# Spreading the float64-to-float32 weight conversion and the head norms over more engines of one Trainium2 core

## The chip, the core and the metric

The kernel runs on one core of one Trainium2 chip. The core has five engines that run their own in-order instruction queues and meet through semaphores: TensorE (PE, matrix products into the accumulator memory PSUM), VectorE (DVE), ScalarE (ACT), GpSimd (POOL), and SyncE (SP, which here only issues DMAs). The metric is device time in microseconds (us) from one execution; the kernel before was run three times, with a median of 1260.8 us.

## What is computed

A linear attention with random features, and a gated feed-forward layer on its result. Cut to what matters:

```python
# q, k, v: 8 batches x 8 heads x 576 tokens x 64, omega: 128 x 64
def phi(x):
    proj = np.einsum('bhsd,md->bhsm', x, omega)
    sq = np.sum(x * x, axis=-1, keepdims=True) / 2.0
    h = proj - sq
    h = h - np.max(h, axis=-1, keepdims=True)
    return np.exp(h) / np.sqrt(m)
q_p, k_p = phi(q * scale), phi(k * scale)
kv = np.einsum('bhsm,bhsd->bhmd', k_p, v)
num = np.einsum('bhsm,bhmd->bhsd', q_p, kv)
den = np.einsum('bhsm,bhm->bhs', q_p, np.sum(k_p, axis=2))[..., None] + 1e-06
x = (num / den)                      # 4608 tokens x 512 after a transpose
gate = 1.0 / (1.0 + np.exp(-(x @ w_gate)))     # w_gate, w_val: 512 x 1536
val = x @ w_val
out = gate * val @ w_out                       # w_out: 1536 x 512
```

The three weight matrices come as float64. The kernel gets them as pairs of 32-bit words and turns each pair into one float32 itself, on the chip.

## The kernel before

**Precision.** Most matrix products are made of three: each float32 operand is split into a rounded part `hi` and a remainder `lo` (`split`, L68: ScalarE writes `hi` at L70, VectorE or GpSimd subtracts at L71), and TensorE multiplies lo with hi, hi with lo, and hi with hi.

**Stages.** While the attention runs (all tasks of `attention`, L681), TensorE's queue also holds the products of a first pass over the feed-forward layer (`first_pass`, L227, products `gv` at L247) for four of the twelve column tiles of the gate and value weights. When attention ends, the rest of the first pass follows, and then `second_pass` (L394, products `gw` at L351) does the other columns with a seven-product scheme for 2 x 2 blocks. Last, `last` (L443, products `po` at L465) multiplies by the output weights.

**Weight conversion.** `from_float64` (L74) converts one half tile, 128 partitions x 512 numbers. `bits` holds the low and high words side by side, so `lo` and `hi` are read with a step of two words. `a` is a scratch tile that both halves of a weight tile share, and `t` receives the float32. VectorE has six instructions (L78, L81, L85, L88, L92, L94): clear the sign, clamp, shift the exponent and mantissa into place, put back the sign, cut out the power of two (into `a`), and multiply the low word by it (back into `a`). GpSimd's add at L96 joins the parts. There are 36 such halves: 8 for the first pass (tiles named `e`), 22 for the weights of the second pass and the output (tiles `c`), and 6 for the last three weight tiles, which are converted after attention has ended because there was no room before (tiles `late`). For `c` and `late` tiles four GpSimd subtractions (L180) follow, and SyncE stores the result to DRAM (`w32`, L181), from where `unit` (L192) loads it later (L199, L200) and splits it (L214 on ScalarE, L215).

**Head norms.** `norms` (L493) loads one tile of 128 tokens x 512 (8 heads x 64) at a time, ScalarE squares it into `x2` (L501, two buffers), and VectorE sums each head's 64 squares (L503, 128 x 512 to 128 x 8). There are 72 such tiles. The scaled sums (`sq`, L507) enter `hm` (L556), from which keys take their bias `nb` (L574) for the exponentials `kpk` (L587), and queries take `sub` (L613) and `h` (L615), which TensorE transposes (`pt`, L626).

**Order.** Program code yields in turns from tasks, and a scheduler then sets each engine's order from that program and its own estimate of times; what is wrapped in `pin` (most of the second pass) keeps program order. SyncE's loads and stores share one in-order queue: the loads of attention inputs `raw` (L519), which wait until a buffer's split is done, the loads `xr` of attention output (L224), of weight words (L144), the stores L181, and the loads of `unit`.

Of the kernel before, what the change touches and what calls it, by code (L numbers as in the profile page):

```python
# [9 lines left out]
F32 = mybir.dt.float32  # L10
F32R = mybir.dt.float32r
AF = mybir.ActivationFunctionType
ALU = mybir.AluOpType
AX = mybir.AxisListType
U32 = mybir.dt.uint32

B, H, S, D = 8, 8, 576, 64
# [56 lines left out]
def from_float64(nc, t, a, bits):  # L74


    lo, hi = bits[:, :, 0], bits[:, :, 1]
    nc.vector.tensor_scalar(out=a, in0=hi, scalar1=0x7FFFFFFF, scalar2=None, op0=ALU.bitwise_and)  # L78

    f = a.bitcast(F32)  # L80
    nc.vector.tensor_scalar(  # L81
        out=f, in0=f, scalar1=LARGEST, scalar2=LEAST, op0=ALU.min, op1=ALU.max
    )

    nc.vector.tensor_scalar(  # L85
        out=t, in0=a, scalar1=3, scalar2=0x3FFFFFFF, op0=ALU.logical_shift_left, op1=ALU.bitwise_and
    )
    nc.vector.scalar_tensor_tensor(  # L88
        out=t, in0=hi, scalar=0xC0000000, in1=t, op0=ALU.bitwise_and, op1=ALU.bitwise_or
    )  # L90

    nc.vector.tensor_scalar(out=a, in0=t, scalar1=0xFF800000, scalar2=None, op0=ALU.bitwise_and)  # L92
    r = a.bitcast(F32)
    nc.vector.scalar_tensor_tensor(out=r, in0=lo, scalar=2.0**-52, in1=r, op0=ALU.mult, op1=ALU.mult)  # L94
    x = t.bitcast(F32)
    nc.gpsimd.tensor_tensor(out=x, in0=x, in1=r, op=ALU.add)  # L96


# [1 line left out]
def attn_glu_kernel(ctx: ExitStack, tc, qT, kT, qn, kn, va, om, ident, w, out):  # L100
    nc = tc.nc
# [36 lines left out]
    def converted(cv, i):  # L138


        raw = [cv[:, (1 + h) * 2 * WP : (2 + h) * 2 * WP] for h in range(2)]
        for h in range(2):
            o = i + h * WP
            nc.sync.dma_start(out=raw[h].rearrange("p (n two) -> p n two", two=2), in_=w[:, o : o + WP, :])  # L144
        yield
        for h in range(2):
            from_float64(
                nc, cv[:, h * WP : (h + 1) * WP], cv[:, 6 * WP :],
                raw[h].rearrange("p (n two) -> p n two", two=2),
            )  # L150
            yield
# [336 lines left out]
    def span(name, b):  # L488

        g = GROUPS[name][b]  # L490
        return g[0][0], g[-1][-1] + 1

    def norms(pool, name, u, b, src):  # L493

        t0, t1 = span(name, b)
        s = pool.tile([P, MID + 1, H], F32, tag="ss", bufs=2, name=f"ss{name}{u}_{b}")[:, : t1 - t0]
        for t in range(t0, t1):
            x = pool.tile([P, DM], F32, tag="nat", bufs=3, name=f"nat{name}{u}_{t}")
            nc.sync.dma_start(out=x, in_=src[u, :, t, :])
            x2 = pool.tile([P, DM], F32, tag="x2", bufs=2, name=f"x2{name}{u}_{t}")  # L500
            nc.scalar.activation(out=x2, in_=x, func=AF.Square)  # L501
            yield
            nc.vector.tensor_reduce(  # L503
                out=s[:, t - t0, :], in_=x2.rearrange("p (h d) -> p h d", d=D), axis=AX.X, op=ALU.add
            )
        sq = pool.tile([P, MID + 1, H], F32, tag="sq", bufs=6, name=f"sq{name}{u}_{b}")
        nc.vector.tensor_scalar(  # L507
            out=sq[:, : t1 - t0], in0=s, scalar1=SCALE * SCALE / 2.0, scalar2=None, op0=ALU.mult
        )
        sqs[name, u, b] = sq  # L510
        yield
# [158 lines left out]
    for u in range(U):  # L670
        for b in range(2):
            for n, x in (("k", kn), ("q", qn)):
                for p in range(NP):
                    if p == 1:
                        tasks.append((("n" + n, u, b), (), lambda pool, a=(n, u, b, x): norms(pool, *a)))
                    needs = (("k", u, p, b - 1),) if n == "k" and b else (("k", u, p, b), ("q", u - 1 + b, p, 1 - b)) if n == "q" else ()
                    make = keys if n == "k" else queries
                    tasks.append(((n, u, p, b), needs, lambda pool, a=(u, p, b), f=make: f(pool, *a)))
# [32 lines left out]
    with tc.tile_pool(name="early", bufs=1) as early:  # L711
# [39 lines left out]
        for n, _ in enumerate(gates):  # L751
# [9 lines left out]
            if n == left - 2 * NE:  # L761
                parts = operands(0)
                x = next(parts)
# [114 lines left out]
```

## Time and profile before

| | |
|---|---|
| three runs | 1260.8, 1253.29, 1263.12 us; median 1260.8 |
| the profiled execution's own time | 1255.57 us |
| its span, first to last instruction | 1253.8 us |
| share of the span: PE, DVE, ACT, POOL | 93%, 70%, 42%, 43% |
| mean granted TensorE clock | 0.967 of full |

The profile has three parts that matter here: tables of busy time in stretches of the span, lists of who waited for whom (an engine's idle time, put down to what ended it last), and the instructions in order of time. A busy TensorE is not one at its best: when its granted clock is lower, the same products are busy for longer. VectorE's 70% is a mean over stages that differ: the prediction reads it by stage.

### The profile page before, as it was taken

What the parts mean: (1) busy time and instruction counts of PE and PEld (TensorE: products, weight loads), DVE (VectorE), ACT (ScalarE), POOL (GpSimd) and SP (SyncE); (2) the same over time, 40 slices, a digit from 0 to 9 for tenths busy, and PEclk for the clock granted to TensorE, in tenths of its full rate; (3) what the DMA queues carried; (4) which work ended last, traced back from release to release, by engine and by line L of the source; (5) the groups of instructions that cost most, each with busy time, mean ns of one, the idle gap of its engine ahead of it and who ended that gap; (6) DMA issues with size and microseconds to landing.
All of it is one profiled execution on the core that took longest, in us unless ns stands there. A gap on an engine that the chain in (4) does not pass through costs nothing.

```text
span 1253.8 us, 23995 instructions
## 1 busy us (share of the span) xinstructions
PE 1171.8 (93%) x8828; PEld 1108.1 (88%) x8828; DVE 881.2 (70%) x1907; ACT 529.1 (42%) x1164; POOL 544.2 (43%) x599
## 2 busy tenths in 40 slices
PE   5789889999898999999799999999999899999998
PEld 5689868788877888788799999999998899999998
DVE  4889877999786565574866656665658786777773
ACT  5556755655444554331533222222224343434331
POOL 2554443755465232154366666666666311111110
PEclk7799889999898999999799999999999999999999
DMA  7666767775565330266532333233327676666662
GB/s 252 211 199 218 242 219 225 273 258 190 196 223 174 109 117 26 93 234 219 177 121 119 123 123 123 89 122 152 123 89 273 212 230 203 192 187 187 198 186 95
DMA packets 104950, 219.43 MB, mean 175 GB/s; under 512 B 11136, under 2 KB 42112, under 8 KB 103040
## 3 DMA queue, kind: packets, MB, share of 16 engines
q1 hardware_dynamic: 87984, 198.94, 47.9%
q10 hardware_dynamic: 16848, 18.95, 4.4%
q8 instruction: 70, 1.15, 0.4%
q14 instruction: 48, 0.39, 0.1%
HBM read 141.82 MB, written 76.02 MB: 174 GB/s over the span
## 4 chain that ended last, share of the span: by engine, by line
PE 48%; POOL 3%; issue 2%; DVE 2%; DMA 2%; ACT 0%; SPq 0%; DVEq 0%; POOLq 0%; ACTq 0%
PE gw L351 27%; PE po L465 21%; POOL late L180 1%; DMA ye<-ye 1%; DMA u<-w 1%; POOL late L96 1%; POOL xe L71 0%; DMA yl<-yl 0%; DMA yr<-yl 0%; POOL xl L296 0%; POOL u L215 0%; DVE yl L71 0%; DVE u L209 0%; POOL yl L391 0%; SPq L224 0%
## 5 line engine op out<-in xcount | busy, mean ns | idle before, releaser
L351 PE MATMUL gw<-xl,u 128*128 128x256 f32 x3024 | 366.4, 284 | 11.0 <-ACT xl L293 4.0
L351 PEld LDWEIGHTS gw<-xl,u 128*128 128x128 f32 x3024 | 364.3, 191 | 13.1 <-ACT xl L293 4.2
L465 PE MATMUL po<-u,yh 128*128 128x256 f32 x1512 | 272.5, 283 | 0.0
L465 PEld LDWEIGHTS po<-u,yh 128*128 128x128 f32 x1512 | 234.8, 191 | 0.0
L465 PE MATMUL po<-u,yl 128*128 128x256 f32 x756 | 214.1, 283 | 3.2 <-DVE yl L71 3.2
L247 PE MATMUL gv<-xe,wh 128*128 128x512 f32 (+1 forms) x640 | 199.9, 387 | 4.1 <-POOL xe L71 4.0
L70 ACT ACTIVATE yh<-yr 128x896 fp32r<-128x896 f32 x108 | 100.6, 951 | 156.5 <-PE po L465 88.2
L465 PEld LDWEIGHTS po<-u,yl 128*128 128x128 f32 x756 | 144.4, 191 | 3.8 <-DVE yl L71 3.8
L247 PEld LDWEIGHTS gv<-xe,wh 128*128 128x128 f32 x640 | 116.0, 193 | 22.1 <-POOL xe L71 6.6
L71 POOL TENSOR_TENSOR yl<-yr,yh 128x896 fp32r<-128x896 f32 x17 | 37.9, 2231 | 215.3 <-PE po L465 140.3
L247 PE MATMUL gv<-xe,wl 128*128 128x512 f32 (+1 forms) x320 | 124.5, 391 | 1.7 <-ACT xe L70 1.1
L71 DVE TENSOR_TENSOR yl<-yr,yh 128x896 fp32r<-128x896 f32 x91 | 99.5, 1102 | 37.8 <-PE po L465 24.9
L331 DVE TENSOR_TENSOR u<-gw,p 128x256 f32<-128x256 f32 x144 | 60.7, 422 | 60.6 <-PE gw L351 52.0
L595 PEld LDWEIGHTS pkv<-v,kpk 128*128 128x128 f32 x512 | 78.9, 212 | 24.4 <-ACT kpk L587 21.8
L595 PE MATMUL pkv<-v,kpk 128*128 128x66 f32 x512 | 85.7, 293 | 15.5 <-ACT kpk L587 14.3
L71 POOL TENSOR_TENSOR lok<-rawk,hik 128x256 fp32r<-128x256 f32 (+1 forms) x80 | 54.6, 700 | 96.4 <-ACT hik L70 96.2
L71 POOL TENSOR_TENSOR loq<-rawq,hiq 128x256 fp32r<-128x256 f32 (+1 forms) x80 | 57.2, 724 | 73.0 <-ACT hiq L70 72.3
L456 DVE TENSOR_TENSOR yr<-yr 128x128 f32<-128x128 f32 x144 | 64.8, 484 | 28.1 <-DMA yr<-ye 27.5
L71 POOL TENSOR_TENSOR xe<-xr,xe 128x512 fp32r<-128x512 f32 (+1 forms) x40 | 49.9, 1265 | 60.3 <-ACT xe L70 56.5
L587 ACT ACTIVATE kpk<-ppk,nb 128x128 f32<-128x128 f32 x256 | 69.6, 390 | 14.7 <-DVE nb L574 14.5
L638 PE MATMUL pnq<-kv,qpq 128*128 128x66 f32 (+1 forms) x640 | 71.1, 267 | 1.2 <-ACT qpq L628 1.2
L638 PEld LDWEIGHTS pnq<-kv,qpq 128*128 128x128 f32 (+1 forms) x640 | 67.3, 183 | 5.1 <-ACT qpq L628 3.1
(116 smaller groups left out, 2175.5 us busy)
## 6 DMA issues: line engine op xcount, KB each, us to landing
yl<-yl SPq DMA_DIRECT2D x36, 896.0 KB, 3.9
yr<-yl SPq DMA_DIRECT2D x72, 448.0 KB, 3.5
xr<-xT SPq DMA_DIRECT2D x68, 256.0 KB, 4.1
c<-w SPq DMA_DIRECT2D x22, 512.0 KB, 5.2
w<-c SPq DMA_DIRECT2D x11, 1024.0 KB, 5.0
v<-va SPq DMA_DIRECT2D x32, 330.0 KB, 3.5
natk<-kn SPq DMA_DIRECT2D x36, 256.0 KB, 4.4
natq<-qn SPq DMA_DIRECT2D x36, 256.0 KB, 3.8
```

The lines of the kernel that those rows point to most:

```text
L70: nc.scalar.activation(out=hi, in_=x, func=AF.Copy)
L71: (lo_engine or nc.vector).tensor_tensor(out=lo, in0=x, in1=hi.bitcast(F32), op=ALU.subtract)
L96: nc.gpsimd.tensor_tensor(out=x, in0=x, in1=r, op=ALU.add)
L180: nc.gpsimd.tensor_tensor(out=o, in0=x, in1=y, op=ALU.subtract)
L247: nc.tensor.matmul(gv, lhsT=u[:, s], rhs=v, start=(m == 0), stop=(m == 3 * KC - 1))
L331: return nc.vector.tensor_tensor(out=o, in0=a, in1=b, op=ALU.add)
L351: nc.tensor.matmul(o, lhsT=u[:, k, s], rhs=v[:, kc, :], start=(first and m == 0), stop=(m == 5), skip_group_check=not first,)
L456: nc.vector.tensor_tensor(out=raw[:, o], in0=raw[:, a], in1=raw[:, b], op=op)
L465: nc.tensor.matmul(o, lhsT=u[:, i, :], rhs=v[:, k, :], start=(j + m == 0 and n in (1, 6, 5, 4)), stop=(j == NPAIR - 1 and m == 2), skip_gr ...
L587: nc.scalar.activation(out=kp[t][:, h, :], in_=pp[:, 2 * i + h, :], func=AF.Exp, bias=nb[:, t - t0, h : h + 1], scale=SCALE,)
L595: nc.tensor.matmul(pkv[:, h, :], lhsT=kp[b * MID + i][:, h, :], rhs=v[:, i, h, :], start=(i == 0), stop=(i == MID),)
L638: nc.tensor.matmul(pn[r, 2 * i + h, :], lhsT=qp[:, 2 * i + h, r], rhs=kvs[u, p, bb][:, h, :], start=True, stop=True,)
```

## The change

Three edits.

1. In `from_float64`, the sign is cleared by ScalarE (the function Abs on the word read as float32) instead of VectorE.
2. In the same place, the multiplication of the low word by the power of two becomes two instructions: ScalarE converts and scales the low word in place (L94), GpSimd multiplies (L95), and its add (L96) follows.
3. In `norms`, GpSimd first adds the second 32 squares of each head to the first 32 (L504, 128 x 8 x 32, in place), and VectorE sums the 32 that are left (L505).

```diff
     lo, hi = bits[:, :, 0], bits[:, :, 1]
-    nc.vector.tensor_scalar(out=a, in0=hi, scalar1=0x7FFFFFFF, scalar2=None, op0=ALU.bitwise_and)
+    nc.scalar.activation(out=a.bitcast(F32), in_=hi.bitcast(F32), func=AF.Abs)
...
     nc.vector.tensor_scalar(out=a, in0=t, scalar1=0xFF800000, scalar2=None, op0=ALU.bitwise_and)
-    r = a.bitcast(F32)
-    nc.vector.scalar_tensor_tensor(out=r, in0=lo, scalar=2.0**-52, in1=r, op0=ALU.mult, op1=ALU.mult)
-    x = t.bitcast(F32)
+    r, small, x = a.bitcast(F32), lo.bitcast(F32), t.bitcast(F32)
+    nc.scalar.activation(out=small, in_=lo, func=AF.Copy, scale=2.0**-52)
+    nc.gpsimd.tensor_tensor(out=r, in0=small, in1=r, op=ALU.mult)
     nc.gpsimd.tensor_tensor(out=x, in0=x, in1=r, op=ALU.add)
...
-            nc.vector.tensor_reduce(
-                out=s[:, t - t0, :], in_=x2.rearrange("p (h d) -> p h d", d=D), axis=AX.X, op=ALU.add
-            )
+            x2 = x2.rearrange("p (h two d) -> p h two d", two=2, d=D // 2)
+            nc.gpsimd.tensor_tensor(out=x2[:, :, 0], in0=x2[:, :, 0], in1=x2[:, :, 1], op=ALU.add)
+            nc.vector.tensor_reduce(out=s[:, t - t0, :], in_=x2[:, :, 0], axis=AX.X, op=ALU.add)
```

The number of products on TensorE, of DMAs and of table loads stays what it was. The scheduler gives every engine a new order, though, since its estimates of times change. Two places show what that means.

The first is GpSimd's queue at the start of the program. `lok_1_0` is the remainder of keys of head pair 1 from tile 0 on, `x2k_0` the squares of key tile 0. Before:

```order
L71 TENSOR_TENSOR lok_1_0_117<-rawk_1_0_91,hik_1_0_116 128x256
L71 TENSOR_TENSOR lok_1_2_121<-rawk_1_0_91,hik_1_2_120 128x256
L71 TENSOR_TENSOR lok_1_4_125<-rawk_1_0_91,hik_1_4_124 128x128
L71 TENSOR_TENSOR lok_0_0_129<-rawk_0_0_84,hik_0_0_128 128x256
L71 TENSOR_TENSOR lok_0_2_133<-rawk_0_0_84,hik_0_2_132 128x256
L71 TENSOR_TENSOR lok_0_4_137<-rawk_0_0_84,hik_0_4_136 128x128
L71 TENSOR_TENSOR lok_2_0_277<-rawk_2_0_263,hik_2_0_276 128x256
```

The same place after:

```order
L504 TENSOR_TENSOR x2k_0_89<-x2k_0_89 128x8x32
L504 TENSOR_TENSOR x2k_1_97<-x2k_1_97 128x8x32
L71 TENSOR_TENSOR lok_1_0_122<-rawk_1_0_91,hik_1_0_121 128x256
L71 TENSOR_TENSOR lok_1_2_126<-rawk_1_0_91,hik_1_2_125 128x256
L71 TENSOR_TENSOR lok_1_4_130<-rawk_1_0_91,hik_1_4_129 128x128
L71 TENSOR_TENSOR lok_0_0_134<-rawk_0_0_84,hik_0_0_133 128x256
L71 TENSOR_TENSOR lok_0_2_138<-rawk_0_0_84,hik_0_2_137 128x256
L504 TENSOR_TENSOR x2k_2_103<-x2k_2_103 128x8x32
L504 TENSOR_TENSOR x2k_3_109<-x2k_3_109 128x8x32
L504 TENSOR_TENSOR x2k_4_115<-x2k_4_115 128x8x32
L71 TENSOR_TENSOR lok_0_4_142<-rawk_0_0_84,hik_0_4_141 128x128
```

Two additions of squares now stand ahead of the first remainder that TensorE needs, and three more behind it, ahead of the sums of the first group of keys.

The second place is GpSimd's queue between the end of attention and the second pass, where the last three weight tiles (three buffers of the tile `late`) are converted and the last inputs of the first pass (`xe`) are split. Before, from the second half of the second weight tile on:

```order
L71 TENSOR_TENSOR xe_2_7582<-xr_0_7435,xe_2_7582 128x512
L71 TENSOR_TENSOR xe_3_7585<-xr_0_7435,xe_3_7585 128x512
L96 TENSOR_TENSOR late_7247<-late_7247 128x512
L180 TENSOR_TENSOR late_7247<-late_7247 128x256 x3
L96 TENSOR_TENSOR late_7248<-late_7248 128x512
L180 TENSOR_TENSOR late_7247<-late_7247 128x256
L96 TENSOR_TENSOR late_7248<-late_7248 128x512
L180 TENSOR_TENSOR late_7248<-late_7248 128x256 x4
```

The same place after:

```order
L95 TENSOR_TENSOR late_7350<-late_7350 128x512
L71 TENSOR_TENSOR xe_1_7687<-xr_0_7542,xe_1_7687 128x512
L95 TENSOR_TENSOR late_7349<-late_7349 128x512
L96 TENSOR_TENSOR late_7350<-late_7350 128x512
L96 TENSOR_TENSOR late_7349<-late_7349 128x512
L71 TENSOR_TENSOR xe_2_7690<-xr_0_7542,xe_2_7690 128x512
L180 TENSOR_TENSOR late_7349<-late_7349 128x256 x3
L71 TENSOR_TENSOR xe_3_7693<-xr_0_7542,xe_3_7693 128x512
L180 TENSOR_TENSOR late_7349<-late_7349 128x256
L95 TENSOR_TENSOR late_7350<-late_7350 128x512
L96 TENSOR_TENSOR late_7350<-late_7350 128x512
L180 TENSOR_TENSOR late_7350<-late_7350 128x256 x4
```

The multiplications L95 are new in the queue, and the last splits `xe_2` and `xe_3` stand behind more of the conversion than before.

## The prediction

> **What bounds the kernel now.** I read busy time by stage first, then who TensorE waits for, then groups of instructions, and the instructions in order of time where the change touches a chain. The stretches are the start, attention with most conversions, its fullest part once more by itself, attention's rest, the change to the second pass, and the rest. The columns are length, then PE, weight loads, DVE, ACT, POOL with their counts, the granted clock, and DMA:
>
> ```profile
> 0.00:40.00 40.00, 24.01 (x122) 22.42 (x123) 22.34 (x47) 23.70 (x70) 14.72 (x24) 0.81 0.75 257
> 40.00:320.00 280.00, 251.59 (x1813) 227.85 (x1813) 242.44 (x599) 162.52 (x444) 142.04 (x161) 0.94 0.69 224
> 220.00:320.00 100.00, 95.62 (x682) 83.56 (x681) 94.07 (x220) 57.50 (x161) 60.30 (x69) 1.00 0.70 238
> 320.00:540.00 220.00, 201.39 (x1363) 175.94 (x1362) 137.53 (x361) 101.42 (x279) 80.90 (x96) 0.96 0.41 134
> 540.00:612.00 72.00, 64.34 (x281) 53.16 (x280) 47.78 (x65) 20.90 (x33) 30.06 (x27) 0.91 0.61 211
> 612.00:1253.80 641.80, 630.49 (x5256) 628.75 (x5254) 431.08 (x837) 220.60 (x342) 276.44 (x292) 1.00 0.48 158
> ```
>
> From 612 us on nothing of the change runs, so the time can only move by the moment at which the second pass starts. Between 40 and 320 us VectorE is the second busiest, 242.4 of 280 (87%), beside TensorE's 251.6 (90%). In 40 to 540 us TensorE is not busy for 500 - 251.6 - 201.4 = 47 us. Who ended those waits (us in total, times, longest):
>
> ```profile
> PE ptq L626 <- DVE hq L615: 12.2, 12, 2.7
> PE pkv L595 <- ACT kpk L587: 8.4, 11, 1.5
> PE ptq L626 <- DVE subq L613: 5.2, 6, 1.6
> PE gv L247 <- POOL xe L71: 4.0, 6, 1.2
> PE pxq L655 <- DVE xq L649: 3.7, 4, 1.0
> ```
>
> With twelve smaller rows this is 23.8 us for VectorE, 16.8 for ScalarE and 5.4 for GpSimd. So even a VectorE that never makes TensorE wait gives 23.8 us, and any gain in clock on top.
>
> **What VectorE loses.** Groups by shape (busy, mean ns of one | idle before); the 22 `c` halves stand for the 36, and the two other names have the same instructions:
>
> ```profile
> L78 DVE TENSOR_SCALAR c<-c 128x512 uint32<-128x512 uint32 x22 | 12.6, 579 | 3.5 <-POOL c L96 3.5
> L88 DVE SCALAR_TENSOR_TENSOR c<-c 128x512 uint32<-128x512 uint32 x22 | 16.7, 760 | 0.2
> L94 DVE SCALAR_TENSOR_TENSOR c<-c 128x512 f32<-128x512 uint32 x22 | 15.6, 709 | 0.1
> L503 DVE TENSOR_REDUCE ssk<-x2k 128x8 f32<-128x512 f32 x36 | 24.3, 676 | 9.9 <-ACT x2k L501 9.7
> L552 DVE TENSOR_REDUCE mxk<-ppk 128x2 f32<-128x256 f32 x16 | 6.6, 415 | 0.0
> L501 ACT ACTIVATE x2k<-natk 128x512 f32<-128x512 f32 x36 | 22.6, 628 | 11.6 <-DMA natk<-kn 6.5 <-DVE ssk L503 2.8 <-DVE ye L275 1.5
> L96 POOL TENSOR_TENSOR c<-c 128x512 f32<-128x512 f32 x22 | 29.2, 1328 | 48.5 <-DVE c L94 28.1 <-DVE invq L647 15.3 <-DVE hmq L556 4.0
> L180 POOL TENSOR_TENSOR c<-c 128x256 f32<-128x256 f32 x44 | 35.6, 822 | 1.3
> L390 POOL TENSOR_TENSOR yl<-yl,gl 128x256 f32<-128x256 f32 x36 | 35.2, 979 | 0.0
> ```
>
> Conversion: 36 x (0.579 + 0.709) = 46 us leave VectorE. Norms: 72 sums fall from 0.676 to about 0.415 us, the mean of a reduction over half as many numbers (L552; it reads PSUM, so this is the nearest row and not the same one; the ends are 0.34, half of 0.676, and 0.676 itself if the row did not get cheaper by size): 72 x 0.261 = 19 us. Together 65 us, of which 23 halves and 63 sums, 30 + 16 = 46 us, lie in 40 to 320 us (instructions of L94 and L503 counted there).
>
> **What ScalarE gains.** Two instructions a half, neither shown in the trace. The square L501 of the same size takes 0.628 us; the ends are that, since nothing says that they are cheaper, and twice that, if reading every second word cost double. On VectorE the step costs little: L94 reads `lo` with it in 0.709, L503 as many numbers without it in 0.676. I take 0.63: 72 x 0.63 = 45 us, 29 of them in 40 to 320 us: ScalarE goes from 162.5 to 191 (68%).
>
> **What GpSimd gains.** L95 as L96: 36 x 1.328 = 48 us (up to 36 x 1.7 if the step costs as L390 over L180 does). L504: 72 additions of 128x256 at 0.822 (L180; high end L390's 0.979): 59 us. In 40 to 320 us that is 23 x 1.328 + 63 x 0.822 = 82 us on 142: 224, or 80%. GpSimd becomes the second busiest engine there, and takes VectorE's place.
>
> **What GpSimd does to VectorE.** While GpSimd runs, VectorE's conversion steps are slow. In order of time (start, length), the first L88 of the `late` tiles with GpSimd idle, and a later one beside two GpSimd instructions; ahead of them the durations of L78 (shortest, median, longest in ns):
>
> ```profile
> L78 DVE TENSOR_SCALAR c<-c x22: 413/421/1491, 104.8 to 377.0; 128x512 uint32<-128x512 uint32 x22
> 546.39 0.69 DVE L88 SCALAR_TENSOR_TENSOR late<-late 128x512 uint32<-128x512 uint32 x1
> 559.95 1.77 DVE L88 SCALAR_TENSOR_TENSOR late<-late 128x512 uint32<-128x512 uint32 x1
> 559.71 1.47 POOL L71 TENSOR_TENSOR xe<-xr,xe 128x512 fp32r<-128x512 f32 x1
> 561.14 1.18 POOL L180 TENSOR_TENSOR late<-late 128x256 f32<-128x256 f32 x1
> ```
>
> Of the four instructions that stay on VectorE three are of L78's kind and one is L88. Their mean lies above the undisturbed length by 0.579 - 0.421 = 0.16 and 0.760 - 0.69 = 0.07: 36 x (3 x 0.16 + 0.07) = 20 us of excess with GpSimd half busy. At 1.6 times its load I take 32, so VectorE's relief is 65 - 12 = 53 us. The ends are no growth, and all of these at the ratio 1.77 / 0.69 = 2.6: 36 x (3 x 0.421 + 0.69) = 70 us would grow by 1.6 x 70 - 20 = 92, which eats the relief whole.
>
> *A rule against the change.* The Trainium skill, Perfetto Trace Analysis, section Optimizing Scalar/DVE Operations, says that moving work between GpSimd and VectorE might not help, since they share a port to SBUF that a VectorE instruction may lock. The trace agrees that they hold each other up (0.69 against 1.77 us above). By the rule alone the relief would be nothing; by the mean rows it is 53 us.
>
> **Does the relief reach TensorE?** By load alone VectorE's 23.8 us of waits should shrink with it. The same list for 220 to 320 us (first row) and for 320 to 540 us (the next three), and the longest wait of SyncE's queue for GpSimd in the first 320 us:
>
> ```profile
> PE ptq L626 <- DVE hq L615: 2.4, 2, 2.1
> ...
> PE ptq L626 <- DVE hq L615: 3.7, 6, 0.9
> PE ptq L626 <- DVE subq L613: 3.1, 4, 1.1
> PE pxq L655 <- DVE xq L649: 1.8, 2, 1.0
> ...
> SPq L519 <- POOL lok L71: 27.5, 13, 6.6
> ```
>
> Where VectorE is fullest (94%) it holds TensorE 2.4 us in 100; where it is busy 63%, 8.6 us in 220, or 3.9 in 100. So these waits do not follow its load. They are the latency of a chain (maximum, bias, subtraction, transposition), and the change shortens no link of it, only the queue ahead. I take a quarter, -6 us, between 0 and -23.8. ScalarE's and GpSimd's waits, 16.8 + 5.4, I let grow with their loads (x1.18, x1.58): 3.0 + 3.1, say +6 us, between 0 and their doubling, +22. The next inputs' loads, which wait for GpSimd's splits already, are within that high end. So this stage comes out even.
>
> **The start.** TensorE's first products and the first key sums pass through GpSimd:
>
> ```profile
> 7.31 3.21 POOL L71 TENSOR_TENSOR lok<-rawk,hik 128x256 fp32r<-128x256 f32 x5 [6.87 <-ACT hik L70]
> 12.41 0.63 ACT L501 ACTIVATE x2k<-natk 128x512 f32<-128x512 f32 x1 [1.09 <-DMA natk<-kn]
> 13.08 0.69 DVE L503 TENSOR_REDUCE ssk<-x2k 128x8 f32<-128x512 f32 x1 [0.64 <-ACT x2k L501]
> 16.59 2.24 PE L595 MATMUL pkv<-v,kpk 128*128 128x66 f32 x8 [3.29 <-ACT kpk L587]
> ```
>
> In the new order the second addition stands ahead of the five splits and ends near 9.1 (the second square ends at 8.3), so these end at 12.3 instead of 10.5; three additions make it 14.8, and the last sum ends at 15.2 instead of 13.8. TensorE's wait at 16.59 grows by that: +1.4 us (0 to +2).
>
> **The change to the second pass.** The chain of work that ended last runs here through the late conversions on GpSimd, the store behind them on SyncE, and the loads that stand behind that store:
>
> ```profile
> 548.35 1.41 POOL L96 TENSOR_TENSOR late<-late 128x512 f32<-128x512 f32 x1 [6.83 <-DVE late L94]
> 577.99 2.95 POOL L180 TENSOR_TENSOR late<-late 128x256 f32<-128x256 f32 x4
> 580.97 0.32 SPq L181 DMA_DIRECT2D w<-late  x1
> 584.05 0.49 SPq L199 DMA_DIRECT2D u<-w  x1
> 589.75 0.85 ACT L214 ACTIVATE u<-u 128x768 fp32r<-128x768 f32 x1 [11.93 <-DMA u<-w]
> 600.91 0.58 PE L351 MATMUL gw<-xl,u 128*128 128x256 f32 x1 [4.03 <-ACT xl L293]
> ```
>
> From 548.35 to 580.94 GpSimd is busy for 24.2 us (6 L96, 12 L180, 4 splits) and idle for 8.4. Six L95 at 1.41 are 8.5 us more. If they all fell into the gaps, the store would stay at 580.97. But two gaps are waits for VectorE, and the second half of a tile cannot start (Abs writes `a`) before L96 of the first has read `a`, which now comes one GpSimd instruction later. Placing the new order with these lengths by hand, I lose about 3.7 us between the first halves and none at the end; the chain then ends near 584.2. SyncE's store and all loads behind it shift, and so does the second pass: +3.3 us (0 to +8.5).
>
> **Sum.** -6 + 6 + 1.4 + 3.3 = about +5 us on 1255.6, so 1260. The profiled execution is 5.2 us below the median of 1260.8, from which the same sum gives 1265; I take 1262. One per cent, 12.6 us, is about what a measurement of this kernel can tell from no change.
>
> **Rivals.**
>
> *VectorE was the limit.* For it: 87% over 280 us, and VectorE named first among the waits. Then its 23.8 us go, ScalarE and GpSimd add little because their queues had room (58% and 51%), and TensorE's clock, 0.94 in that stage, rises: 0.02 on 252 us is 5 more. 1260.8 - 24 - 5 + 5 = 1237. Against it: the waits that do not follow its load. Chance 0.28.
>
> *GpSimd becomes the limit of attention.* Its place is 80 to 320 us, where splits (`lok`, `loq`, `xe`) queue behind additions and multiplications, and raw buffers come free later. It decides once GpSimd's load passes TensorE's own 90%: at 80% by the means, it does so if L504 costs 0.979 and L95 1.7 (224 + 10 + 9 = 243 of 280, 87%) and the two engines' blocking adds the rest. Then the doubling of ScalarE's and GpSimd's waits, +22, no gain, and +5: 1288. Chance 0.15.
>
> *The relief is eaten by the two engines' mutual blocking.* VectorE stays at its load, its waits stay, and GpSimd and ScalarE add 6 to 12 us, the late stage its 8.5: about 1260.8 + 17 = 1278. The rule cited above would make it this one. Chance 0.08.
>
> *No change worth seeing*, the forecast: 1262, itself between 1250 and 1272. Chance 0.49.
>
> **Range and chances.** Faster by over 1% is the first rival, 0.28; slower the next two, 0.23; within 1% 0.49. To leave out no more than 2 in 10, the low end goes to 1240, into the first rival, and the high end to 1282, between the two slower ones.
>
> **What would show it.** VectorE's busy time in 40 to 320 us near 205, ScalarE's near 191, GpSimd's near 224; L504 near 0.82 us, L95 near 1.33, the new sum near 0.415; the first `pkv` 1.4 us later; TensorE's waits for VectorE still above 15 us; the last store L181 some 48 us behind attention's last product as before, plus 3. I am wrong if those waits vanish, if GpSimd leads TensorE's waits, or if the late chain ends no later than before.

## The result, and the profile after

| | before | after |
|---|---|---|
| median, four runs each | 1261.96 us | 1297.0 us |
| lowest and highest | 1253.29, 1267.33 | 1295.07, 1305.97 |
| profiled execution, its span | 1255.57, 1253.8 | 1297.45, 1295.6 |
| mean granted TensorE clock | 0.967 | 0.953 |

The change makes the kernel slower: ratio 1.0298, 95% interval 1.0223 to 1.0374, some 37 us. The forecast was no change worth seeing, 1262 us, between 1240 and 1282; the measured time lies above all of that.

The stretches of the kernel after come first, columns as in the prediction (length; PE, weight loads, DVE, ACT, POOL with counts; granted clock; DMA share; GB/s). The last row is the whole of attention, from the start to its last product (the transposition at L655):

```profile
0.00:40.00 40.00, 22.60 (x110) 21.53 (x110) 17.96 (x39) 22.23 (x60) 21.31 (x33) 0.83 0.74 245
40.00:320.00 280.00, 230.72 (x1596) 211.65 (x1594) 196.87 (x504) 170.06 (x450) 189.32 (x224) 0.88 0.63 204
320.00:540.00 220.00, 202.16 (x1402) 178.03 (x1402) 136.26 (x360) 115.12 (x317) 102.34 (x121) 0.96 0.43 141
...
0.00:560.10 560.10, 473.27 (x3229) 426.61 (x3230) 363.35 (x940) 313.35 (x837) 312.97 (x377) 0.91 0.54 177
```

The same attention in the kernel before:

```profile
0.00:522.50 522.50, 460.43 (x3231) 413.05 (x3231) 396.60 (x1000) 279.14 (x777) 229.63 (x275) 0.94 0.58 190
```

Attention grew by 37.6 us of the 41.8 between the two spans. (The profiled execution before is 6 us faster than its median, the one after is at its median, so this pair shows a few us more than the loss.) The counts of TensorE's products are the same, so this is the same work. VectorE was busy for 33 us less in it, ScalarE for 34 more and GpSimd for 83 more. Between 40 and 320 us VectorE fell from 87% to 70%, and TensorE beside it from 90% to 82%: the engine that was relieved did not let the other one run. The 37.6 us have two parts. TensorE is busy for 473.3 us instead of 460.4 with the same products (12.8 us, its granted clock 0.91 instead of 0.94), and it stands idle for 86.8 us instead of 62.1 (24.7 us). Who ended those waits in attention, and below that what VectorE and ScalarE waited for (us in total, times, longest):

```profile
PE ptq L626 <- DVE hq L615: 21.8, 18, 3.5
PE pkv L595 <- ACT kpk L587: 17.8, 13, 3.5
PE ppk L547 <- POOL lok L71: 11.7, 2, 10.2
PE ppq L547 <- DVE hmq L556: 7.5, 1, 7.5
PE pnq L638 <- ACT qpq L628: 5.1, 3, 4.1
PE gv L247 <- POOL xe L71: 4.9, 6, 3.0
...
PE pxq L655 <- DVE invq L647: 3.9, 1, 3.9
...
DVE ssq L505 <- POOL x2q L504: 31.8, 16, 5.3
...
DVE ssk L505 <- POOL x2k L504: 19.0, 12, 4.0
...
ACT c L78 <- POOL c L96: 18.1, 6, 7.2
```

With the smaller rows, over the whole of attention in both kernels, VectorE is named for 41.5 us (before 23.8), ScalarE for 26.4 (22.7), GpSimd for 18.5 (14.0). Most of the growth has VectorE's name. But VectorE itself now stands for 31.8 + 19.0 = 51 us at its sums (L505) until GpSimd has added the halves (L504): the engine with less work is late because it stands behind another one's queue. Instructions of the kernel after in order of time (start, length, engine, line, then idle time and what ended it) show the start, one such place, and the last store of a converted weight:

```profile
15.29 0.42 DVE L505 TENSOR_REDUCE ssk<-x2k 128x8 f32<-128x256 f32 x1 [0.22 <-POOL x2k L504]
...
18.66 2.24 PE L595 MATMUL pkv<-v,kpk 128*128 128x66 f32 x8 [1.90 <-ACT kpk L587]
...
261.77 1.76 POOL L95 TENSOR_TENSOR c<-c 128x512 f32<-128x512 f32 x1
263.49 1.27 POOL L71 TENSOR_TENSOR xe<-xr,xe 128x512 fp32r<-128x512 f32 x1
264.72 1.27 POOL L96 TENSOR_TENSOR c<-c 128x512 f32<-128x512 f32 x1
265.95 0.72 POOL L504 TENSOR_TENSOR x2q<-x2q 128x256 f32<-128x256 f32 x1
...
266.70 0.42 DVE L505 TENSOR_REDUCE ssq<-x2q 128x8 f32<-128x256 f32 x1 [4.35 <-POOL x2q L504]
...
268.33 0.17 DVE L647 RECIPROCAL invq<-denq 128x2 f32<-128x2 f32 x1
...
269.16 0.45 PE L655 MATMUL pxq<-id_sb,xq 128*128 128x128 f32 x1 [3.86 <-DVE invq L647]
...
622.06 0.32 SPq L181 DMA_DIRECT2D w<-late  x1
```

An addition of 0.72 us stands in GpSimd's queue behind 4.2 us of weight conversion and input splits. VectorE waits 4.35 us for it, with the reciprocal that TensorE needs queued behind the sum, and so TensorE waits 3.86 us. No engine is full over the stage; for these few microseconds GpSimd is.

The lengths of single instructions came out as forecast. Groups by shape of the kernel after (busy, mean ns of one | idle before):

```profile
L504 POOL TENSOR_TENSOR x2k<-x2k 128x256 f32<-128x256 f32 x36 | 26.9, 755 | 25.2 <-ACT x2k L501 25.1
L505 DVE TENSOR_REDUCE ssk<-x2k 128x8 f32<-128x256 f32 x36 | 14.7, 411 | 19.1 <-POOL x2k L504 19.0
L95 POOL TENSOR_TENSOR c<-c 128x512 f32<-128x512 f32 x22 | 29.5, 1343 | 36.1 <-DVE c L92 12.7 <-DVE invq L647 8.9 <-DVE hmq L556 6.3
L78 ACT ACTIVATE c<-c 128x512 f32<-128x512 f32 x22 | 14.8, 671 | 20.7 <-POOL c L96 18.1 <-DMA c<-w 2.0 <-ACT xsq L661 0.6
L94 ACT ACTIVATE c<-c 128x512 f32<-128x512 uint32 x22 | 14.4, 670 | 0.0
L88 DVE SCALAR_TENSOR_TENSOR c<-c 128x512 uint32<-128x512 uint32 x22 | 19.1, 867 | 0.3
```

L504 took 0.755 us (forecast 0.822), L505 0.411 (0.415), L95 1.343 (1.328), ScalarE's two steps 0.67 each (0.63). What failed is not a duration.

### The profile page after: what moved, and what is told of

Same layout as the page of the kernel before. It is cut to its first block, busy times and chain, and to the rows that moved or that the text cites. A ratio compares the mean times of both kernels' runs of the same rounds, so it can differ in the third digit from the quotient of the medians.

```text
span 1295.6 us, 24087 instructions
## 1 busy us (share of the span) xinstructions
PE 1185.3 (91%) x8828; PEld 1121.3 (87%) x8828; DVE 838.3 (65%) x1835; ACT 569.2 (44%) x1236; POOL 635.9 (49%) x707
## 4 chain that ended last, share of the span: by engine, by line
PE 46%; POOL 3%; issue 2%; DMA 2%; DVE 1%; SPq 0%; ACT 0%; DVEq 0%; POOLq 0%; ACTq 0%
PE gw L351 26%; PE po L465 19%; DMA u<-w 0%; POOL late L95 0%; POOL late L180 0%; DMA ye<-ye 0%; DMA yl<-yl 0%; POOL late L96 0%; POOL xe L71 0%; DVE yl L71 0%; DMA yr<-yl 0%; POOL xl L296 0%; POOL u L215 0%; SPq L224 0%; DVE u L209 0%
## 5 line engine op out<-in xcount | busy, mean ns | idle before, releaser
L351 PE MATMUL gw<-xl,u 128*128 128x256 f32 x3024 | 366.8, 284 | 11.3 <-ACT xl L293 4.1
L351 PEld LDWEIGHTS gw<-xl,u 128*128 128x128 f32 x3024 | 364.7, 191 | 13.3 <-ACT xl L293 4.3
L247 PE MATMUL gv<-xe,wh 128*128 128x512 f32 (+1 forms) x640 | 204.2, 396 | 6.6 <-POOL xe L71 6.6
L71 POOL TENSOR_TENSOR yl<-yr,yh 128x896 fp32r<-128x896 f32 x17 | 38.4, 2256 | 215.0 <-PE po L465 157.1
L247 PEld LDWEIGHTS gv<-xe,wh 128*128 128x128 f32 x640 | 119.3, 198 | 25.1 <-POOL xe L71 9.2
L247 PE MATMUL gv<-xe,wl 128*128 128x512 f32 (+1 forms) x320 | 128.6, 404 | 5.0 <-ACT xe L70 2.3
L71 DVE TENSOR_TENSOR yl<-yr,yh 128x896 fp32r<-128x896 f32 x91 | 102.7, 1145 | 27.9 <-ACT yh L70 15.3
L595 PEld LDWEIGHTS pkv<-v,kpk 128*128 128x128 f32 x512 | 82.8, 222 | 27.3 <-ACT kpk L587 24.7
L595 PE MATMUL pkv<-v,kpk 128*128 128x66 f32 x512 | 88.9, 300 | 19.1 <-ACT kpk L587 17.8
L71 POOL TENSOR_TENSOR loq<-rawq,hiq 128x256 fp32r<-128x256 f32 (+1 forms) x80 | 55.3, 701 | 82.1 <-ACT hiq L70 81.7
L456 DVE TENSOR_TENSOR yr<-yr 128x128 f32<-128x128 f32 x144 | 60.6, 455 | 40.5 <-DMA yr<-ye 40.0
L638 PEld LDWEIGHTS pnq<-kv,qpq 128*128 128x128 f32 (+1 forms) x640 | 70.7, 189 | 9.6 <-ACT qpq L628 7.1
L638 PE MATMUL pnq<-kv,qpq 128*128 128x66 f32 (+1 forms) x640 | 74.1, 272 | 5.1 <-ACT qpq L628 5.1
L247 PEld LDWEIGHTS gv<-xe,wl 128*128 128x128 f32 x320 | 63.1, 198 | 13.6 <-ACT xe L70 2.5
L71 POOL TENSOR_TENSOR lok<-rawk,hik 128x256 fp32r<-128x256 f32 (+1 forms) x80 | 54.9, 701 | 40.6 <-ACT hik L70 40.5
```

The lines of the kernel that those rows point to most:

```text
L71: (lo_engine or nc.vector).tensor_tensor(out=lo, in0=x, in1=hi.bitcast(F32), op=ALU.subtract)
L247: nc.tensor.matmul(gv, lhsT=u[:, s], rhs=v, start=(m == 0), stop=(m == 3 * KC - 1))
L351: nc.tensor.matmul(o, lhsT=u[:, k, s], rhs=v[:, kc, :], start=(first and m == 0), stop=(m == 5), skip_group_check=not first,)
L456: nc.vector.tensor_tensor(out=raw[:, o], in0=raw[:, a], in1=raw[:, b], op=op)
L595: nc.tensor.matmul(pkv[:, h, :], lhsT=kp[b * MID + i][:, h, :], rhs=v[:, i, h, :], start=(i == 0), stop=(i == MID),)
L638: nc.tensor.matmul(pn[r, 2 * i + h, :], lhsT=qp[:, 2 * i + h, r], rhs=kvs[u, p, bb][:, h, :], start=True, stop=True,)
```

## The experiments

The theories, with the letters that the expectations use. **L**: GpSimd's added work as such costs the time, since all that other engines need from GpSimd stands behind it in its queue. **H**: the hand-off costs it, that is VectorE standing at its sums. **S**: the scheduler's new order costs it, whatever was added. Two came later. **Q**: GpSimd's load costs because TensorE's own input splits (`lok`, `loq`, L71) stand in that queue. **C**: the edits cost more together than one by one. **W** and **G** stand for the change's own waits, and for a price of the load by other ways than those splits. Executions of one kernel scatter by up to 0.8% to either side (the kernel before: 1250.4 to 1271.6 us in the 100 executions beside these experiments), so prices are read from the recorded ratios with their 95% intervals, and a single profile only for what it shows of waits. A recorded ratio is not the quotient of the two medians printed beside it; the two differ by up to 0.25%, some 3 us. A ratio of 1.001 is 1.26 us.

**The edits one by one.** Each of the first four kernels is the kernel before with some of the change's edits. Norms alone (edit 3):

```diff
-            nc.vector.tensor_reduce(
-                out=s[:, t - t0, :], in_=x2.rearrange("p (h d) -> p h d", d=D), axis=AX.X, op=ALU.add
-            )
+            x2 = x2.rearrange("p (h two d) -> p h two d", two=2, d=D // 2)
+            nc.gpsimd.tensor_tensor(out=x2[:, :, 0], in0=x2[:, :, 0], in1=x2[:, :, 1], op=ALU.add)
+            nc.vector.tensor_reduce(out=s[:, t - t0, :], in_=x2[:, :, 0], axis=AX.X, op=ALU.add)
```

> The third edit alone (head norms), the conversion as before. Theory H (hand-off): VectorE's queue stands still at sums that wait for GpSimd's additions, 51 us of it in the changed kernel; then this edit alone makes most of the loss, 1262 + 20 to 30 = 1282 to 1292, with VectorE's waits for L504 above 30 us. Theory L (load): what costs is GpSimd's added work in proportion, 53 of 102 us: 1262 + 18 = 1280. Theory C (both together): only the backlog that both edits build up on GpSimd costs, then each alone is near 1262.

Measured: 1279.8 against 1260.3 us, ratio 1.0172 (1.0101 to 1.0244), +22 us. By the ratios more than half of the whole loss comes with this edit. The time is L's 1280. The 22 us would fit H's 20 to 30 as well, but VectorE's waits at its sums are 27.5 us, where H says above 30.

Both edits of the conversion, without the norms:

```diff
-    nc.vector.tensor_scalar(out=a, in0=hi, scalar1=0x7FFFFFFF, scalar2=None, op0=ALU.bitwise_and)
+    nc.scalar.activation(out=a.bitcast(F32), in_=hi.bitcast(F32), func=AF.Abs)
...
-    r = a.bitcast(F32)
-    nc.vector.scalar_tensor_tensor(out=r, in0=lo, scalar=2.0**-52, in1=r, op0=ALU.mult, op1=ALU.mult)
-    x = t.bitcast(F32)
+    r, small, x = a.bitcast(F32), lo.bitcast(F32), t.bitcast(F32)
+    nc.scalar.activation(out=small, in_=lo, func=AF.Copy, scale=2.0**-52)
+    nc.gpsimd.tensor_tensor(out=r, in0=small, in1=r, op=ALU.mult)
```

> The first two edits alone (conversion), the norms as before. H: ScalarE waits for GpSimd's last add of the half before, 33 us in the changed kernel, and VectorE for ScalarE; part of it costs TensorE, 1262 + 5 to 12 = 1267 to 1274. L: 49 of 102 us of GpSimd's added work, 1262 + 17 = 1279. C: near 1262.

Measured: 1267.9, ratio 1.0069 (1.0041 to 1.0098), +9 us. This is within H's range, and L's price in proportion to the work, 17 us, is missed: GpSimd has 33 us more to do in attention and the time grows by half of what L says. Norms and conversion, 22 + 9 = 31 us, lie within the interval of the whole change (28 to 47).

The first `-`/`+` pair of that diff alone, and then the rest of it alone:

> The first edit alone (the sign cleared on ScalarE); GpSimd has the work of before. H: VectorE loses 21 us of work and gains a wait for ScalarE, which waits for GpSimd's add: 1258 to 1266. L: no work is added to GpSimd, so not slower than before, 1255 to 1262.

> The second edit alone (low word scaled on ScalarE, multiplied on GpSimd). H: nothing but GpSimd waits for these two, so little cost: 1258 to 1266. L: 49 of 102 us of GpSimd's added work: 1262 + 17 = 1279.

Measured: 1.0053 (1.0014 to 1.0093), +7 us, and 1.0147 (1.0096 to 1.0198), +18 us. The medians are 1268.0 and 1278.7 us. L is wrong on the first (no work is added to GpSimd, and the kernel is slower) and right on the second; H, with 1258 to 1266 for each, is just missed on the first and far off on the second. The second edit alone costs more than both together, by 10 us. A price of one edit to a few microseconds is not to be had here; each edit also gives another order, and that this is the reason is not shown.

**Only GpSimd's load, or only the hand-off.** The next kernels keep VectorE's whole sum. The first adds a tiny GpSimd instruction a tile, of 0.25 us, whose result nobody reads:

```diff
+            nc.gpsimd.tensor_scalar(out=om_sb[:, :1], in0=x[:, :1], scalar1=1.0, scalar2=None, op0=ALU.mult)
```

> The kernel before plus 72 tiny GpSimd instructions (128 x 1, one for each norm tile, written to a tile that nobody reads). No work to speak of and no wait for it, but the scheduler deals out another order. Theory S (order): the new order alone moves the time, by 5 us or more either way. Theories H and L: 1260, within 4 us.

Measured: 1.0008 (0.9976 to 1.0040). This other order cost nothing; it is one order of many.

The second adds as much GpSimd work as edit 3 does, also read by nobody:

```diff
+            nc.gpsimd.tensor_tensor(out=om_sb, in0=x[:, : DM // 2], in1=x[:, DM // 2 :], op=ALU.add)
```

> The kernel before plus GpSimd's 72 additions of the third edit (128 x 256), made on the unsquared tile and written where nobody reads; VectorE's sums stay whole and wait for nothing new. L (GpSimd's work as such, through its splits and through the slowing of VectorE): 1260 + 15 to 20. H (the hand-off): most of the loss is gone, 1260 + 0 to 6.

Measured: 1274.7 against 1260.95, ratio 1.0133 (1.0082 to 1.0184), +17 us. Half of the added instructions, by the groups by shape (the other half, from `natq`, is alike; it waits for its input alone):

```profile
L503 POOL TENSOR_TENSOR om_sb<-natk 128x256 f32<-128x256 f32 x36 | 28.7, 796 | 15.9 <-DMA natk<-kn 14.9
```

57 us of work whose result no instruction reads cost 17 us (10 to 23), as L said. Edit 3 with the same work costs 22 (13 to 31). One thing does wait for the added instructions: the load of a later tile into the same `nat` buffer, in SyncE's queue, for 6.0 us in all. It adds nothing to SyncE's standing at these loads, which is 51 us in attention here and 70 in the kernel before.

The third puts a tiny GpSimd instruction between the square and the whole sum, which VectorE has to wait for:

```diff
+            nc.gpsimd.tensor_scalar(out=x2[:, :1], in0=x2[:, :1], scalar1=1.0, scalar2=None, op0=ALU.mult)
```

> The kernel before with a tiny GpSimd instruction (128 x 1, times one, in place on the squares) between the square and VectorE's whole sum: no work for GpSimd, but VectorE's sum now waits for a place in GpSimd's queue. H: 1260 + 10 to 20, with VectorE's waits for that line above 20 us. L: 1260, within 4.

Measured: 1263.7, ratio 1.0028 (1.0000 to 1.0056), +3.5 us, and VectorE does stand at the sums (who VectorE waited for in that kernel):

```profile
DVE ssk L504 <- POOL x2k L503: 13.4, 9, 3.4
DVE ssq L504 <- POOL x2q L503: 9.6, 6, 2.3
```

So 23 us of standing at the sums cost at most some 7 us of time. With the norms alone VectorE stands for hardly longer, and the price is 22 us:

```profile
DVE ssk L505 <- POOL x2k L504: 18.1, 15, 3.8
DVE ssq L505 <- POOL x2q L504: 9.4, 5, 4.5
```

As the main cause H falls.

The fourth is edit 3 with the addition on VectorE itself (`nc.vector.tensor_tensor` in place of `nc.gpsimd.tensor_tensor`):

> The third edit with its addition on VectorE instead of GpSimd: no hand-off and no work for GpSimd, but VectorE does 72 x (0.42 + 0.41 - 0.68), about 11 us, more than before. H and L: 1260 + 2 to 6. If VectorE's load were what TensorE waits for, the full 11.

Measured: 1247.6, ratio 0.9896 (0.9859 to 0.9934), 13 us faster than before, with two instructions a tile on VectorE instead of one:

```profile
L504 DVE TENSOR_TENSOR x2k<-x2k 128x256 f32<-128x256 f32 x36 | 19.3, 540 | 6.2 <-ACT x2k L501 6.2
...
L505 DVE TENSOR_REDUCE ssk<-x2k 128x8 f32<-128x256 f32 x36 | 14.5, 408 | 0.2
```

VectorE does 0.54 + 0.41 = 0.95 us for a tile of keys instead of 0.676, some 17 us more over all tiles, and the kernel is faster, which no theory had foreseen. VectorE's load was no limit.

**How the load costs.** The line of GpSimd load, twice (114 us):

> As e6, with two such additions for each tile, 114 us of GpSimd's work that nobody waits for instead of 57. Theory L, now in the form Q (TensorE's split inputs come later because they queue behind other work on GpSimd): the loss grows with the dose, 1260 + 30 to 45. Theory S (another order, of whatever kind): no dose, 1260 + 5 to 20 as in e6.

Measured: 1301.4 against 1258.7, ratio 1.0364 (1.0325 to 1.0402), +46 us, the upper end of L's 30 to 45; S, which has no dose and at most 20, does not fit. Doubling the load more than doubles its price. Its attention:

```profile
0.00:564.70 564.70, 481.84 (x3229) 432.43 (x3230) 409.95 (x1000) 279.38 (x777) 341.00 (x419) 0.90 0.53 176
```

This kernel has nothing of the change, and it shows the change's pattern, only larger: TensorE's busy time up by 21 us at a clock of 0.90, its idle time up by 21 to 83, with GpSimd busy for 60% of attention. The `nat` buffers do not explain it: SyncE's loads now stand for 34 us until the second addition has read its tile, but for 65 us in all at these loads, after 70 in the kernel before:

```profile
SPq L499 <- POOL om_sb L504: 33.9, 28, 2.5
```

To take TensorE's input splits out of GpSimd's queue, they go to VectorE; here in the kernel after:

```diff
-                split(nc, hi, lo, raw[:, o : o + nt * P], lo_engine=nc.gpsimd)
+                split(nc, hi, lo, raw[:, o : o + nt * P])
```

> The changed kernel, with the subtractions that make lok and loq on VectorE instead of GpSimd (160 instructions: GpSimd loses 110 us, VectorE gains about 66, to more work than in the kernel before). All of the change's waits between engines stay. Q: the inputs of TensorE no longer queue on GpSimd, 1297 - 25 to 45 = 1252 to 1272. Theory W (the change's own waits, ScalarE and VectorE standing at what GpSimd makes): 1285 or more, since these waits stay and VectorE is fuller.

Measured: 1279.8, ratio 1.0173 (1.0134 to 1.0212). More than half of the loss stays, although GpSimd is now less busy in attention (210 us) than in the kernel before. The time lies between what Q and what W says, and bears out neither.

The conversion's edits together with the norms' addition on VectorE:

> The two conversion edits with the norm's addition on VectorE (e2 and e8 together). If e2's loss (8 us) and e8's gain (13 us) are effects of work and add: 1253 to 1258. If e8's gain is a lucky order that another edit upsets: 1265 to 1275.

Measured: 1.0077 (1.0044 to 1.0109), +10 us: the conversion's +9 is there, the 13 us that the addition on VectorE had gained are not. That is what the expectation says for a lucky order.

The kernel before with each sum replaced by two sums of four heads, which gives VectorE more to do and GpSimd nothing:

```diff
+            x2 = x2.rearrange("p (h d) -> p h d", d=D)
+            for i in (slice(0, H // 2), slice(H // 2, H)):
+                nc.vector.tensor_reduce(out=s[:, t - t0, i], in_=x2[:, i], axis=AX.X, op=ALU.add)
```

> The kernel before with each sum of a norm tile cut into two of four heads on VectorE: as much more VectorE work as in e8 (about 11 us) in equally short instructions, and no second input from SBUF. If short instructions on VectorE are what e8 gains by: 1245 to 1251. If it was the order that e8 happened to get: 1256 to 1268.

Measured: 1244.2, ratio 0.9894 (0.9867 to 0.9922), as fast as short instructions would have it. The sums' groups in it:

```profile
L505 DVE TENSOR_REDUCE ssq<-x2q 128x4 f32<-128x256 f32 x72 | 27.9, 407 | 1.4 <-ACT x2q L501 1.3
L505 DVE TENSOR_REDUCE ssk<-x2k 128x4 f32<-128x256 f32 x72 | 27.5, 405 | 8.1 <-ACT x2k L501 7.9
```

That is 55.4 us busy, where 72 whole sums of 0.676 are 48.7. This kernel and the addition on VectorE are the fastest versions found, and both beat the kernel before and the kernel after.

**Load with the splits elsewhere.** The kernel before with its splits `lok`, `loq` on VectorE, and the same with the doubled GpSimd load:

> The kernel before with lok and loq on VectorE: the control for e10 and e14. GpSimd loses 110 us of work, VectorE gains about 66. Q and the rival G alike give no number for it: near 1260 if VectorE has room, up to 1285 if it has not. What counts is how e10 and e14 stand to it.

> e9's 114 us of GpSimd work that nobody waits for, with lok and loq on VectorE as in e13. Q (the load costs because lok and loq queue behind it): within 10 us of e13. G (GpSimd's load costs by what else it touches: the splits xe, the conversion's last steps, VectorE slowed beside it): e13 + 25 to 45, as e9 stands to before.

Measured: 0.9917 (0.9873 to 0.9960) and 1.0040 (0.9997 to 1.0082). The same 114 us of added work that cost 46 us now cost 1.2%, 16 us, between Q's 10 and G's 25. Attention of the second one:

```profile
0.00:536.70 536.70, 472.67 (x3229) 425.75 (x3230) 447.59 (x1160) 280.51 (x777) 232.41 (x259) 0.91 0.58 185
```

Its GpSimd load of 232 us is that of the kernel before, its VectorE load is 51 us higher, and its time is within half a per cent.

For comparison, load on ScalarE: two copies a tile that nobody reads, 59 us in all:

```diff
+            nc.scalar.activation(out=om_sb, in_=x[:, : DM // 2], func=AF.Copy)
+            nc.scalar.activation(out=om_sb, in_=x[:, : DM // 2], func=AF.Copy)
```

> The kernel before with 144 additional ScalarE copies (128 x 256, two for each norm tile) that nobody waits for, 60 us of work, as much as e6's on GpSimd. ScalarE makes the hi parts of the same splits. If any in-order queue on the way to TensorE costs when it is made fuller: 1260 + 10 to 20. If it is GpSimd's alone: 1260, within 5.

Measured: 1.0056 (1.0025 to 1.0087), +7 us, between the two expectations; as much work on GpSimd cost 17.

Last, the change's parts with the splits on VectorE: the conversion's edits, the norms' edit, and the sums cut in two:

> The two conversion edits with lok and loq on VectorE (against e13). GpSimd has room. W (waits of ScalarE at GpSimd's add, and of VectorE at ScalarE): e13 + 15 to 25 = 1266 to 1276, and most of the 30 us that e10 stands above e13. If GpSimd's queue was all: within 6 of e13.

> The norm edit with lok and loq on VectorE (against e13). Q: GpSimd has room, and little is left of e1's 21 us: within 8 of e13, 1245 to 1259. W: VectorE still stands at sums that wait for GpSimd, e13 + 10 to 15.

> e12 and e13 together: each was about one per cent faster than the kernel before. If the gains add: 1232 to 1240. If they are the same gain, or owed to a lucky order: 1243 to 1255.

Measured: 0.9985 (0.9953 to 1.0017), 0.9941 (0.9905 to 0.9977) and 0.9939 (0.9905 to 0.9972). Against the 0.9917 of the splits alone, the conversion costs 0.7%, as before, and the norms' edit 0.2%, 3 us in place of 22. So the norms' price goes with GpSimd's queue, as Q expects, and the conversion's does not: its 9 us lie between the two expectations for it. The gains of the third kernel do not add. VectorE's waits at its sums in the second:

```profile
DVE ssq L505 <- POOL x2q L504: 2.9, 3, 1.4
DVE ssk L505 <- POOL x2k L504: 2.3, 5, 0.6
```

With an emptier queue the same instructions are there in time: 5.2 us of waiting in place of the 27.5 of the norms alone.

**All of them by GpSimd's load.** GpSimd's busy time in attention by each kernel's profile, and the ratio less one, times 1260 us:

| kernel | GpSimd busy in attention | time against before |
|---|---|---|
| two sums, splits on VectorE | 117 us | -8 us |
| splits on VectorE | 121 | -10 |
| conversion, splits on VectorE | 159 | -2 |
| norms, splits on VectorE | 175 | -7 |
| after, splits on VectorE | 210 | +22 |
| two sums; addition on VectorE | 228; 229 | -13; -13 |
| Abs alone; load on ScalarE | 228; 229 | +7; +7 |
| before | 230 | 0 |
| doubled load, splits on VectorE | 232 | +5 |
| hand-off alone; tiny instruction | 244; 247 | +4; +1 |
| conversion; multiplication alone; conversion with addition on VectorE | 263; 265; 267 | +9; +18; +10 |
| norms alone; load | 278; 283 | +22; +17 |
| after | 313 | +38 |
| doubled load | 341 | +46 |

Above 250 us the time rises with this column, whether the added work is the change's or is read by nobody: about 0.4 us for each us of work (46 / 111 from the last row; 83 x 0.41 = 34 for the kernel after, which lost 38), with single rows between 0.27 (conversion) and 0.5 (multiplication alone). At 228 to 232 us the rows lie anywhere between -13 and +7, since other things differ too, and below that no rise is clear of such scatter, but for one row that stands outside: the kernel after with its splits on VectorE. There TensorE's waits carry ScalarE's name, 39.6 us in attention against 16.4 with the splits on VectorE alone; the largest:

```profile
PE pkv L595 <- ACT kpk L587: 23.6, 12, 4.3
```

## Why the prediction was wrong

| term | predicted | measured |
|---|---|---|
| VectorE's waits, attention | -6 us (0 to -23.8) | +17.7 |
| ScalarE's and GpSimd's waits, attention | +6 (0 to +22) | +8.2, start included |
| TensorE's busy time by its clock | not in the forecast's sum | +12.8 |
| the start (measured: within the rows above) | +1.4 (0 to +2) | +2.1 (first `pkv` 16.59 to 18.66) |
| change to the second pass | +3.3 (0 to +8.5) | +3.6 |

The first three add up to 38.7 us and not to 37.6, since the list of waits before leaves 1.2 us more of the idle time unnamed than the one after.

**What held.** The durations, as shown. The relief is real and was not eaten by slower steps: VectorE's four remaining conversion steps took 93.7 us in all after 91.0, where the forecast allowed for 12 us more. Its busy time in the whole kernel fell from 881.2 to 838.3 us, 43 where the forecast had 53. The change to the second pass: the first product of that pass (L351) starts at 636.7 after 595.5 us, 41.2 later, of which attention is 37.6; the last store L181 follows attention's last product by 62.0 us after 58.5. (The 48 us that the prediction named for this were miscounted; the +3 beside it was right.) From that first product to the end it is 658.9 us after 658.3, so the rest is untouched, as assumed. That VectorE's load in 40 to 320 us is 197 us, near the forecast 205, is partly luck: in these 280 us the kernel after gets through 1,596 of TensorE's products in place of 1,813, and ScalarE (170, forecast 191) and GpSimd (189, forecast 224) stay well below what was named for them. And the reading that TensorE's waits with VectorE's name do not follow VectorE's load was right: three kernels give VectorE 7, 17 and (with the splits) 25 us more to do and are about 1% faster.

**The step that failed** is "So this stage comes out even", by its first term: "the change shortens no link of it, only the queue ahead. I take a quarter, -6 us, between 0 and -23.8". With VectorE's name on them the waits grew by 17.7 us instead. The bound excluded a loss with no reason to do so. The change does not only take work from VectorE's queue, it puts a wait for GpSimd into it 72 times, and what TensorE needs can stand behind that wait, as at 262 us. The prediction named what queues behind GpSimd's new work at the start and at the change to the second pass, and both came within 0.7 us of its sizes; for attention it only scaled waits with loads. None of its three signs of being wrong appeared: VectorE's waits did not vanish, GpSimd does not lead TensorE's list, and the late chain ends later.

That wait alone is not the price, though: with a nearly empty instruction on GpSimd it cost 3.5 us. The runs show GpSimd's added work as the main cause: read by nobody, 57 us cost 17 and 114 us cost 46. For the norms' edit, the larger part of the loss, this is shown from both sides, since it costs 3 us in place of 22 when GpSimd's queue is emptier. For the conversion's 9 us it is not: they stay with the emptier queue, and the Abs step alone, with no work for GpSimd, costs 7. In the kernel with the doubled load the names in TensorE's list are others than in the kernel after (GpSimd 24.9 us, VectorE 31.4), with much the same total of idle time and the same fall of the clock. With the norms alone VectorE's name is on 24.9 us, hardly more than the 23.8 before, and the loss is there all the same. Which engine has its name on the wait was thus no guide to the cause here; whose queue got longer was a better one.

**The clock** was the second omission. The forecast counted a gain of clock in one rival only, and no loss anywhere. A third of attention's growth between the two profiles, 12.8 of 37.6 us, is the same products at a lower granted clock. Other kernels split their growth over the kernel before otherwise:

| attention of | TensorE busy longer | idle longer | clock |
|---|---|---|---|
| tiny instruction | 6.2 us | -6.6 us | 0.93 |
| norms alone | 6.0 | 10.1 | 0.93 |
| load | 11.3 | 6.4 | 0.92 |
| after | 12.8 | 24.7 | 0.91 |
| after, splits on VectorE | 15.5 | 6.6 | 0.90 |
| doubled load | 21.4 | 20.8 | 0.90 |

By these single profiles the clock is half of the doubled load's price and two thirds of the row that stands outside the table above. What lowers it is not shown. It also differs between executions of one kernel: over the whole span, the kernel before had 0.974 in one of 1251.9 us and 0.952 in one of 1271.4. The kernel after had 0.942 to 0.954 in its four; 98 of the 100 of the kernel before lie above that. The fall is real, then, but one pair of profiles does not give its price.

**The rivals.** The second, GpSimd as the limit of attention, named the right engine and place; its 1288 us were 9 short. Its condition was wrong: "It decides once GpSimd's load passes TensorE's own 90%". GpSimd is busy for 68% of 40 to 320 us and 56% of attention, and the doubled load cost 46 us at 60%. Others waited for it long before it was full. The first rival, VectorE as the limit, is refuted by the same three kernels. The third, mutual blocking, fell by its mechanism, 2.7 us of growth. The Trainium skill, Perfetto Trace Analysis, section Optimizing Scalar/DVE Operations, which warned that moving work between GpSimd and VectorE might not help because of their shared port, agrees with the trace in the outcome (ratio 1.0298). The reason that it gives is not where the time went here: VectorE's four steps grew by 2.7 us in all, and GpSimd's add L96 took 1.295 us for a `c` half after 1.328.

**What stays open.** With the splits on VectorE the added load costs a third of what it did. Whether that is because those splits feed TensorE (Q), or because a queue shortened by any 110 us would do, was not told apart: above 250 us the table reads as one rising curve without Q. The kernel after with its splits on VectorE is 22 us slower than before at a GpSimd load of 210 us, where the curve gives nothing and ScalarE's extra work some 7; the costs of the conversion (0.7%) and the norms (0.2%) one by one do not add up to its 2.6% over the splits alone, so there is some effect of both together (C) whose cause was not found; TensorE's waits for ScalarE and the lower clock are where it shows. And 10 us between the multiplication alone and both conversion edits show how far a single price can be off, so the 17 us of the load is less sure than the 46 of its double. The gains of about 1% do not add either: the sums cut in two gain 13 us, the splits on VectorE 10, both together 8. Each such kernel has its own order from the scheduler; whether shorter VectorE instructions or a luckier order gave the 1% was not tried with the order held fixed.

## What to carry to other kernels

Before moving work to an engine that is half idle, list what other engines wait for from it, and price the move by the length of its queue just ahead of those results; a busy share of 50 to 60% was no sign of room here, and an engine that was nearly full had some, since nobody's waits followed its load. The cheapest test is to add the same work to the receiving engine with its result read by nobody: here that one line showed 17 of the norm edit's 22 us. (Look at what the added instruction keeps waiting by reading its input, too.) And where TensorE's products are a fixed number, count the clock beside the idle time.

## What the runs showed of the hardware

TensorE's granted clock did not simply follow the idle time of the stage, though the pair of before (0.94 with 62 us idle in attention) and after (0.91 with 87) looks like it. It was 0.93 with 49.5 us idle (two sums, splits on VectorE) and with 76.7 (multiplication alone), 0.91 with 64.0 (doubled load, splits on VectorE), and 0.94 with 72.0 (conversion). The same 3,230 products were busy for 452 us at 0.96, 460 at 0.94, 473 at 0.91 and 482 at 0.90, a spread of 30 us without one instruction more, and much of the scatter between executions of one kernel goes with the clock as well (kernel before: 1251.9 us at 0.974, 1271.4 at 0.952). The other surprise is the sum in two parts: two reductions of 128x256 at 0.405 us take longer than one of 128x512 at 0.676 (0.81 us), and yet the kernel with them is one of the two fastest.
